# A top-32 attention and a cosine-gated layer: every step from one list with the first twenty units reordered, and the mask made from threshold minus score

## The chip, the cores and the metric

The kernel runs on one core of one Trainium2 chip. The metric is the time of one execution in device microseconds (us), as the median of several runs. The core has a matrix engine (TensorE, PE in the profile; its loads of stationary operands are listed as PEld), a vector engine (VectorE, DVE), a scalar engine (ScalarE, ACT), a general engine (GpSimd, POOL), and a sync engine (SyncE, SP) that here only issues DMAs. Each engine works through its own instructions in order and waits on semaphores for the others.

## The reference

Inputs are q, k and v of shape (8, 8, 576, 64), that is batch, heads, sequence, head size, and two weight matrices of 512 x 2048 and 2048 x 512. All arithmetic is float32. The reference, cut to what matters:

```python
scores = scale * np.matmul(q, k.transpose(0, 1, 3, 2))
kth = np.partition(scores, -32, axis=-1)[..., -32:-31]
scores = np.where(scores >= kth, scores, -1000000000.0)
scores = scores - np.max(scores, axis=-1, keepdims=True)
attn = np.exp(scores)
attn = attn / (np.sum(attn, axis=-1, keepdims=True) + 1e-09)
x = heads_joined(np.matmul(attn, v))      # (4608, 512)
h = x @ w_in                              # (4608, 2048)
return (h * np.cos(h)) @ w_out            # (4608, 512)
```

For each row of scores, only the 32 largest of 576 count; the softmax runs over these.

## The kernel before

**Units and blocks.** The 4608 token rows are cut into 36 blocks of 128. With the heads taken in four pairs, there are 144 units: unit n is block n // 4, head pair n % 4. A unit passes through these steps:

- Scores: PE multiplies q and k (L242), 448 columns into one PSUM tile (`sc`, two buffers) and 128 into a shared one (`rim`). ACT copies both to SBUF as `s` (`take_scores`, L253 and L257).
- Folding: a row's 576 scores are split in halves. DVE forms the maximum of each pair (`rest`, `fold_high`, L267); POOL forms the minimum as sum minus maximum on the integer bit patterns (`low`, L283 and L292). In units 8 to 10 (`BUSY`) DVE makes the minimum directly (`fold_now`, L275).
- Search: DVE takes the eight largest of a row at a time (MAX8, L359) and strikes them out (MATCH_REPLACE8, L364): four rounds on `rest`, two on `low`. Two small reductions merge the lists into the 32nd largest score, the threshold (L347, L352). They are done at the start of the next unit's search.
- Mask: two more small reductions on DVE make the negated threshold and the negated maximum (`bounds`, L372) and the distance of threshold and maximum (`distances`, L379), both between the maxima of the next unit's first round. ACT multiplies the distance by the scale (L386), masks (L388) and exponentiates with a running sum (L396). The mask is the function Prelu: a score minus the threshold stays as it is if it isn't negative, and is multiplied by 2^100 if it is, so that its exponential is zero.
- Sum and reciprocal on DVE (L404, L409).
- Transposition: POOL splits the words of `s` and the reciprocals into 16-bit halves (`split`, L419 and L421, into one buffer), SP writes them to DRAM (L450), and a transposing DMA reads them back into a ring of five (L456). The first four units are transposed by PE instead (`turn`, L438 to L446).

When the four units of a block are there, PE multiplies with v (`values`, L484) and DVE multiplies with the reciprocals (`take_values`, L500, L508), giving the block's x, transposed.

**The second layer, per block.** The first product takes 64 matmuls on PE (`ff1`, L562); ACT copies each PSUM bank twice (`take_first`, L576, L578); POOL reduces to the range of the sine (L598, L607); ACT takes the sine (L617); POOL multiplies (`gate`, L624); the second product takes 16 matmuls (`ff2`, L637); ACT copies the result (L647) and issues its store. A block has two chunks of g and x in SBUF: six buffers for g and three for x.

**Weights.** They arrive as 64-bit words and are decoded on the chip in 32 pieces of 128 x 512: a load of 512 KB (L120) into a buffer of g or x, two passes on ACT (L133, L136), a shift on DVE (L151, two adjacent pieces in one instruction where possible), and an addition on POOL (L160), after which the buffer is free.

**What sets the order.** A Python loop calls `slot` once for each unit, and each engine gets its instructions in the order in which the loop emits them. A slot holds the search of unit i, the mask and exponentials of unit i − 1, the split and transposition of unit i − 2, the scores of one or two units ahead, and pieces of the second layer. Which pieces those are is decided by `feed` from a small table (`plan`) and by tests on counters (`can_first`, `can_second`), which let the first product begin in slot 6 at the earliest and the second in slot 10. The loads of weights are issued on SP's queue in slots 0 to 5 and on ACT's queue in later ones. After the last unit, `drain` and `forward` emit what is left.

Of the kernel before, what the change touches and what calls it, by code (L numbers as in the profile page):

```python
# [17 lines left out]
P = 128  # L18
# [12 lines left out]
def kernel(  # L31
# [63 lines left out]
    BUSY = range(8, 11)  # L95
    ff = {"live": 0, "tick": 0, "now": 0, "end": False, "kind": 0, "half": 0, "open": 0, "late": False}

    wq = {"next": 0, "loaded": deque(), "second": deque(), "third": deque(), "done": 0, "ready": 0}

    def staged(spare=0):  # L100
        return sum(c[2] == spare for k in ("loaded", "second", "third") for c in wq[k])

    def load_weights(n, queue):
        for _ in range(n):
            i = wq["next"]
            if i >= len(chunks):
                return
            src, dst = chunks[i]
            if not DECODE:
                queue.dma_start(out=dst[0][:, dst[1]], in_=src)  # L110
                wq["next"] = wq["done"] = i + 1
                continue
            spare = i < 2 * NC + 10 and i % 2 == 1 and staged(1) < XB
            if spare:
                st = ffw.tile([P, CW, 2], I32, tag="x", name="st", bufs=XB)
            elif staged() + ff["live"] >= CHUNKS:
                return
            else:
                st = ffw.tile([P, CW, 2], I32, tag="g", name="st", bufs=CHUNKS)
            queue.dma_start(out=st.rearrange("p w i -> p (w i)"), in_=src)  # L120
            wq["loaded"].append((st, dst, int(spare)))
            wq["next"] = i + 1

# [3 lines left out]
    def decode_first(n):  # L127


        for _ in range(min(n, len(wq["loaded"]))):  # L130
            st, w, spare = wq["loaded"].popleft()
            lo, hi = st[:, :, 0], st[:, :, 1]
            nc.scalar.activation(  # L133
                out=w[0][:, w[1]], in_=hi.bitcast(F32), func=AF.Prelu, scale=2.0**-111, alpha=2.0**32
            )
            nc.scalar.mul(out=lo, in_=lo.bitcast(U32), mul=2.0**-29)  # L136
            wq["second"].append((st, w, spare))

    def decode_second(n):

        left = min(n, len(wq["second"]))
        while left:
            st, (w, c), spare = wq["second"].popleft()
            wq["third"].append((st, (w, c), spare))
            m = 1
            if left > 1 and wq["second"][0][1][0] is w:
                wq["third"].append(wq["second"].popleft())
                m = 2
            left -= m
            wi = w[:, c : c + m].bitcast(I32)  # L150
            nc.vector.tensor_scalar(  # L151
                out=wi, in0=wi, scalar1=3, scalar2=None, op0=ALU.logical_shift_left
            )

    def decode_third():

        while wq["third"]:
            st, w, _ = wq["third"].pop()
            wi = w[0][:, w[1]].bitcast(I32)
            nc.gpsimd.tensor_tensor(out=wi, in0=wi, in1=st[:, :, 0], op=ALU.add)  # L160
            wq["done"] += 1

# [69 lines left out]
    def scores(u):  # L235
        sc = u["sc"] = ps.tile([P, 2, 512], F32, tag="sc", name="sc", bufs=2)
        for to, k0, k1 in ((sc, 0, SB), (sc_ends[u["n"] % 2], SB, S)):
            for b, q0, rows, r0 in u["parts"]:
                for j in range(2):
                    d = slice(j * D, (j + 1) * D)  # L240
                    st = pairs[b, u["hp"]]
                    nc.tensor.matmul(  # L242
                        to[r0 : r0 + rows, rim_bank(r0, j) if k0 else place(u["hp"], j), 0 : k1 - k0],
                        st["q"][d, q0 : q0 + rows],
                        st["k"][d, k0:k1],
                        start=True,
                        stop=True,
                    )
# [61 lines left out]
    def topk_first(u, w):  # L310

        u["top"] = tops[u["n"] % len(tops)]
        if w:
            merge_first(w)
        if u["n"] not in BUSY:
            fold_sum(u)
        fold_high(u)
        if w:
            merge_second(w)
        if u["n"] in BUSY:  # L320
            fold_now(u)
        topk_round(u, 0, [lambda: bounds(w), lambda: distances(w)] if w else ())

    def topk_round(u, rnd, between=(), ahead=None):
        top, rest, lasts = u["top"], u["rest"], TOPK // 8 - 1
        end = TOPK - 1 - 8 * rnd
        at = top[:, :, end : end - 8 if rnd < lasts else None : -1, 0]
        search(
            at, rest[:, :, HS:S] if rnd == 0 else rest[:, :, 0:HS], rest[:, :, 0:HS], rnd < lasts,
            between if rnd < lasts else (),  # L330
        )
        if rnd < lasts:
            return
        del u["rest"]
        low = u.pop("low")
        for k in range(TOPK // 16):
            more = k < TOPK // 16 - 1
            if ahead and not more:
                ahead()
            search(top[:, :, 1 + 8 * k : 9 + 8 * k, 1], low, low, more, () if more else between)  # L340


# [14 lines left out]
    def search(to, src, rest, more, between=()):  # L357
        for j in range(2):
            nc.vector.max(to[:, j], src[:, j])  # L359
            if between:  # L360
                between[j]()
        if more:
            for j in range(2):
                nc.vector.match_replace(rest[:, j], to[:, j], src[:, j], NEG)  # L364

    def bounds(u):

        top = u.pop("top").rearrange("p j r i -> p j (r i)")
        end = 2 * TOPK
        less = u["less"] = top[:, :, end : end + 2]  # L370
        u["near"] = top[:, :, end - 1 : end + 1]
        nc.vector.tensor_reduce(  # L372
            out=less, in_=top[:, :, end - 2 : end].unsqueeze(3), axis=mybir.AxisListType.X,
            op=ALU.max, negate=True,
        )

    def distances(u):
        u["nd"] = small.tile([P, 2], F32, tag="nd", name="nd")
        nc.vector.tensor_reduce(  # L379
            out=u["nd"], in_=u.pop("near"), axis=mybir.AxisListType.X, op=ALU.add  # L380
        )

    def mask(u):

        s, less = u["s"], u.pop("less")
        nc.scalar.mul(out=u["nd"], in_=u["nd"], mul=SCALE)  # L386
        for j in range(2):
            nc.scalar.activation(  # L388
                out=s[:, j], in_=s[:, j], func=AF.Prelu, bias=less[:, j, 1:2], scale=1.0, alpha=FAR
            )  # L390

    def exponentials(u):
        s, nd = u["s"], u.pop("nd")
        den = u["den"] = dens[u["n"] % len(dens)]
        for j in range(2):
            nc.scalar.activation(  # L396
                out=s[:, j], in_=s[:, j], func=AF.Exp, bias=nd[:, j : j + 1], scale=SCALE,
                accum_out=den[:, j, 0:1],
            )
# [11 lines left out]
    def both(u):  # L411
        return [lambda: sums(u), lambda: reciprocal(u)] if u else ()

    def split(u):


        s = u.pop("s").rearrange("p j k -> p (j k)").bitcast(U16)
        halves = work.tile([P, 2, 2 * S + P], U16, tag="halves", name="halves", bufs=1)
        nc.gpsimd.tensor_copy(out=halves[:, :, 0 : 2 * S], in_=s.rearrange("p (k h) -> p h k", h=2))  # L419
        rden = u.pop("rden").bitcast(U16).rearrange("p (j h) -> p h j", h=2)  # L420
        nc.gpsimd.tensor_copy(  # L421
            out=halves[:, :, 2 * S :].rearrange("p h (j d) -> p h j d", j=2),
            in_=rden.unsqueeze(3).to_broadcast([P, 2, 2, D]),
        )
        u["halves"] = halves
# [4 lines left out]
    def turn(u):  # L430

        s = u.pop("s").rearrange("p j k -> p (j k)")
        pT = u["pT"] = ring[:, u["n"] % RING]
        for half in range(2):
            tt = ps.tile([P, 512], F32, tag="mm", name="tt", bufs=2)
            for c in range(NT):
                at = (half * NT + c) * P
                nc.tensor.transpose(tt[:, c * P : (c + 1) * P], s[:, at : at + P], ident)  # L438
            nc.scalar.copy(out=pT[:, half * NT : (half + 1) * NT], in_=tt.rearrange("p (c q) -> p c q", c=NT))  # L439
        at = 2 * NT * P  # L440
        nc.tensor.transpose(room[0][:, P : 2 * P], s[:, at : at + P], ident)
        rden = u.pop("rden")
# [3 lines left out]
        nc.scalar.copy(out=pT[:, 2 * NT :], in_=rim[:, :, 3 * P :])  # L446
# [43 lines left out]
    def take_values(us):  # L490
# [4 lines left out]
        while i < n:  # L495
            at, h = us[i]["n"] % RING, (hp + i) // 2
            m = 4 if n - i == 4 and at + 4 <= RING else 2 if at + 2 <= RING else 1
            if m > 1:
                o = rim[:, :, 2 * (S - SB) + h * P : 2 * (S - SB) + (h + m // 2) * P]
                nc.vector.tensor_tensor(  # L500
                    out=blk["xT"][:, hp + i : hp + i + m].rearrange("p (h b) q -> p h b q", b=2),
# [409 lines left out]
```

## Time and profile before

| what | value |
|---|---|
| median of 3 runs | 1413.1 us (1413.07 to 1413.49) |
| span of the profiled execution | 1410.6 us |
| busy in the span: PE, PEld | 1354.9 (96%), 976.6 (69%) |
| busy in the span: DVE, ACT, POOL | 1344.2 (95%), 1139.4 (81%), 1164.8 (83%) |
| largest groups on PE: first product L562, second product L637 | 540.0, 524.7 us |
| largest groups on DVE: L359 on `rest`, L364 on `rest` | 478.7, 376.4 us |
| mean of L372, L379 (DVE), x144 each | 140, 141 ns |
| mean of L386, L388, L396 (ACT) | 205, 762, 770 ns |

The profiled execution is one run under the hardware profiler; its span goes from the first instruction to the last, and the median of the runs lies 2.5 us above it. A line of a timeline reads: start in us from the span's start, duration, engine, source line, operation, output and input by the program's names, shapes and count, and in brackets the idle time of the engine before it and what ended that. A line of waits reads: engine and line that waited, what it waited for, the time in total, how often, the longest. "SPq" is a DMA issue on SP's queue.

### The profile page before, as it was taken

The page shows a single profiled execution, that of the slowest core. Times are in us where ns is not written, and L with a number is a line of the kernel's source. Part 1 is how long each engine was busy: PE and PEld are TensorE (multiplying, and loading weights), DVE is VectorE, ACT ScalarE, POOL GpSimd, SP SyncE. Part 2 cuts the span into 40 slices and gives each one's busy share as a digit, 9 for nine tenths or more (in the row PEclk, how much of TensorE's full clock was granted, in tenths as well). Part 3 has the DMA queues.
Part 4 walks back from the last instruction along what each step waited for, and adds up shares of the span by engine and source line. Part 5 has one row for each costly group of instructions (what it writes and reads, how often), then busy time and mean ns, then how long its engine had stood idle before and what let it go on. Part 6 is the DMA issues. An engine that isn't in the chain of part 4 may idle for free.

```text
span 1410.6 us, 32356 instructions
## 1 busy us (share of the span) xinstructions
PE 1354.9 (96%) x11264; PEld 976.6 (69%) x11264; DVE 1344.2 (95%) x5148; ACT 1139.4 (81%) x2043; POOL 1164.8 (83%) x804
## 2 busy tenths in 40 slices
PE   4568999999999999999999999999999999999998
PEld 2445777777777777777777777777777777777775
DVE  7999999999999999999999999999999999999931
ACT  6987888888888888888888888888888888888831
POOL 5778988898888888888888888888888888888810
PEclk7688999999999999999999999999999999999999
DMA  8566876767675575677666677666776666555540
GB/s 274 198 207 180 205 184 165 206 174 192 155 185 151 165 194 158 176 169 194 174 172 160 142 188 186 171 169 161 207 164 168 158 172 172 142 157 148 150 101 15
DMA packets 427443, 240.13 MB, mean 170 GB/s; under 512 B 375952, under 2 KB 392592, under 8 KB 427280
## 3 DMA queue, kind: packets, MB, share of 16 engines
q1 hardware_dynamic: 420720, 224.22, 60.8%
q10 hardware_dynamic: 6560, 13.85, 2.8%
q8 instruction: 88, 1.44, 0.4%
q14 instruction: 75, 0.61, 0.1%
HBM read 45.09 MB, written 101.19 MB: 104 GB/s over the span
## 4 chain that ended last, share of the span: by engine, by line
PE 83%; DVE 10%; ACT 4%; DMA 2%; SPq 0%; issue 0%; ACTq 0%; DVEq 0%
PE o L637 32%; PE mm L562 32%; PE rim L484 10%; PE sc L242 7%; DVE top L359 5%; DVE rest L364 3%; PE rim L242 2%; DMA st<-in_moe_w_in_dram 2%; DVE rest L267 1%; DVE low L364 1%; ACT s L396 1%; ACT st L136 1%; ACT s L388 1%; ACT w_out L133 0%; ACT w_in L133 0%; ACT ring L439 0%
## 5 line engine op out<-in xcount | busy, mean ns | idle before, releaser
L562 PEld LDWEIGHTS mm<-xT,w_in 128*128 128x128 f32 x4608 | 538.3, 192 | 70.8 <-issue 55.7
L562 PE MATMUL mm<-xT,w_in 128*128 128x128 f32 x4608 | 540.0, 276 | 2.2 <-DVE xT L500 1.3
L637 PE MATMUL o<-w_out,g 128*128 128x512 f32 x1152 | 524.7, 599 | 0.0
L359 DVE MAX8 top<-rest 128x8 f32<-128x288 f32 x1152 | 478.7, 451 | 0.0
L364 DVE MATCH_REPLACE8 rest<-top,rest 128x288 f32<-128x288 f32 x864 | 376.4, 443 | 0.0
L637 PEld LDWEIGHTS o<-w_out,g 128*128 128x128 f32 x1152 | 207.7, 190 | 219.5 <-issue 219.2
L419 POOL COPY halves<-s 128x2304 uint16<-128x2304 uint16 x140 | 294.6, 2104 | 51.4 <-ACT s L396 48.2
L359 DVE MAX8 top<-low 128x8 f32<-128x288 f32 x576 | 241.6, 448 | 0.4 <-POOL low L292 0.3
L396 ACT ACTIVATE s<-s,nd 128x576 f32<-128x576 f32 x288 | 220.6, 770 | 0.8
L292 POOL TENSOR_TENSOR low<-low,rest 128x576 int32<-128x576 int32 x141 | 199.3, 1413 | 11.0
L388 ACT ACTIVATE s<-s,top 128x576 f32<-128x576 f32 x288 | 205.7, 762 | 0.0
L283 POOL TENSOR_TENSOR low<-s 128x576 int32<-128x576 int32 x141 | 198.9, 1411 | 5.7 <-ACT s L259 5.7
L386 ACT ACTIVATE nd<-nd 128x2 f32<-128x2 f32 x144 | 29.5, 205 | 177.1 <-DVE nd L379 177.0
L607 POOL TENSOR_TENSOR x<-g,x 128x1024 f32<-128x1024 f32 x68 | 160.8, 2364 | 5.7
L624 POOL TENSOR_TENSOR g<-g,x 128x1024 f32<-128x1024 f32 x68 | 160.8, 2365 | 0.0
L242 PE MATMUL sc<-k,q 64*64 64x448 f32 (+1 forms) x1120 | 145.3, 564 | 15.7 <-DMA k<-in_k_dram 8.6
L484 PE MATMUL rim<-ring,v 128*64 128x128 f32 (+1 forms) x2560 | 138.1, 267 | 0.0
L484 PEld LDWEIGHTS rim<-ring,v 128*64 128x64 f32 x2560 | 129.0, 139 | 6.4 <-issue 5.9
L253 ACT COPY s<-sc 128x896 f32<-128x896 f32 (+1 forms) x144 | 128.5, 892 | 2.7 <-PE sc L242 2.7
L364 DVE MATCH_REPLACE8 low<-top,low 128x288 f32<-128x288 f32 x288 | 125.4, 443 | 0.0
L257 ACT COPY s<-rim 64x256 f32<-64x256 f32 (+1 forms) x280 | 103.0, 368 | 26.6 <-PE rim L484 24.9
L598 POOL TENSOR_SCALAR x<-x 128x1024 f32<-128x1024 int32 x68 | 71.2, 1047 | 63.5 <-ACT x L578 63.5
(56 smaller groups left out, 1272.3 us busy)
## 6 DMA issues: line engine op xcount, KB each, us to landing
rows<-halves SPq DMA_DIRECT2D x140, 640.0 KB, 3.5
out_dram<-ob ACTq DMA_DIRECT2D x36, 256.0 KB, 2.1
q<-in_q_dram SPq DMA_DIRECT2D x31, 288.0 KB, 4.3
st<-in_moe_w_in_dram SPq DMA_DIRECT2D x16, 512.0 KB, 6.9
v<-in_v_dram SPq DMA_DIRECT2D x32, 256.0 KB, 4.3
k<-in_k_dram SPq DMA_DIRECT2D x31, 144.0 KB, 4.2
k<-in_k_dram SPq DMA_DIRECT2D x32, 128.0 KB, 4.5
st<-in_moe_w_out_dram SPq DMA_DIRECT2D x8, 512.0 KB, 5.1
```

Of the source, the lines that this page charges most:

```text
L242: nc.tensor.matmul(to[r0 : r0 + rows, rim_bank(r0, j) if k0 else place(u["hp"], j), 0 : k1 - k0], st["q"][d, q0 : q0 + rows], st["k"][d, k ...
L283: nc.gpsimd.tensor_tensor(out=u["low"].bitcast(I32), in0=s[:, :, 0:HS], in1=s[:, :, HS:S], op=ALU.add)
L292: nc.gpsimd.tensor_tensor(out=low, in0=low, in1=u["rest"][:, :, HS:S].bitcast(I32), op=ALU.subtract)
L359: nc.vector.max(to[:, j], src[:, j])
L364: nc.vector.match_replace(rest[:, j], to[:, j], src[:, j], NEG)
L388: nc.scalar.activation(out=s[:, j], in_=s[:, j], func=AF.Prelu, bias=less[:, j, 1:2], scale=1.0, alpha=FAR)
L396: nc.scalar.activation(out=s[:, j], in_=s[:, j], func=AF.Exp, bias=nd[:, j : j + 1], scale=SCALE, accum_out=den[:, j, 0:1],)
L419: nc.gpsimd.tensor_copy(out=halves[:, :, 0 : 2 * S], in_=s.rearrange("p (k h) -> p h k", h=2))
L484: nc.tensor.matmul(to[d, r], lhsT, rhs, start=(bank, j) not in begun, stop=c == NT - 1 and u in us[-2:] and r0 + rows == P,)
L562: nc.tensor.matmul(mm[:, at : at + w], w_in[f // FC][:, c, (f % FC) * P : (f % FC + 1) * P], blk["xT"][:, c], start=c == 0, stop=c == NC - 1,)
L607: nc.gpsimd.tensor_tensor(out=x, in0=g, in1=x, op=ALU.subtract)
L637: nc.tensor.matmul(o, g[:, at : at + P], w_out[f], start=f == 0, stop=f == NF - 1)
```

## The change

The procedure that chose the order (`slot`, `plan`, `feed`, `can_first`, `can_second`, `drain`, `forward`) is gone. In its place stands one literal list of steps, which a loop calls one after the other; each token names a step and its unit, block or weight piece. `Sa.8` and `Sb.8` are the two parts of unit 8's scores, `K` the copies, `fs`, `fl`, `P0`, `P0b` the folds, `R0` to `R3`, `Q0`, `Q1` the rounds of the search, `M`, `E`, `C` the mask, the exponentials, and sum and reciprocal, `sp1`, `sp2`, `wr`, `tr` the split, write and transposition, `T1` to `T3e` those on PE, `V.4.8` and `X.4.8` the values of units 4 to 7 and their taking, `F1.b.i` and `F2.b.j` the eighths of block b's first and second product, `B1`, `A0`, `A`, `N`, `G` what lies between them, `L`, `D1`, `D2`, `D3` the load and the three decoding steps of a weight piece.

From unit 20 on the list gives PE the same instructions in the same order as before. In the first twenty units the order is new: among other things, the values of block 0 stand in the middle of slot 7 (before: in slot 5, with the first product in slot 6); the first three eighths of block 0's second product stand before the values of block 1 (before: behind them); the split of a unit may stand right behind its exponentials; units 15 and 17 are scored before units 14 and 16. All weight loads are issued on SP's queue, among the writes and transposing DMAs of units 4 to 10. Each weight piece is shifted on its own: 32 shifts of 512 columns instead of 13 of 1024 and 6 of 512.

The mask is Prelu of threshold minus score: negative for the scores that stay, which are multiplied by 2^-100, while the others stay as they are; the exponential's scale undoes both. `bounds` is not needed for it and is gone, `distances` subtracts, and the multiplication of the distance stands behind the masks.

The diff, cut to its core:

```diff
-    def bounds(u):
-        top = u.pop("top").rearrange("p j r i -> p j (r i)")
-        ...
-        nc.vector.tensor_reduce(
-            out=less, in_=top[:, :, end - 2 : end].unsqueeze(3), axis=mybir.AxisListType.X,
-            op=ALU.max, negate=True,
-        )
     def distances(u):
+        top = u["top"]
         u["nd"] = small.tile([P, 2], F32, tag="nd", name="nd")
-        nc.vector.tensor_reduce(
-            out=u["nd"], in_=u.pop("near"), axis=mybir.AxisListType.X, op=ALU.add
+        nc.vector.tensor_tensor(
+            out=u["nd"], in0=top[:, :, TOPK - 1, 1], in1=top[:, :, TOPK - 1, 0], op=ALU.subtract
         )
     def mask(u):
-        s, less = u["s"], u.pop("less")
-        nc.scalar.mul(out=u["nd"], in_=u["nd"], mul=SCALE)
+        s, top = u["s"], u.pop("top")
         for j in range(2):
             nc.scalar.activation(
-                out=s[:, j], in_=s[:, j], func=AF.Prelu, bias=less[:, j, 1:2], scale=1.0, alpha=FAR
+                out=s[:, j], in_=s[:, j], func=AF.Prelu, bias=top[:, j, TOPK - 1, 1:2], scale=-1.0,
+                alpha=1.0 / FAR,
             )
+        nc.scalar.mul(out=u["nd"], in_=u["nd"], mul=SCALE)
     def exponentials(u):
         ...
-                out=s[:, j], in_=s[:, j], func=AF.Exp, bias=nd[:, j : j + 1], scale=SCALE,
+                out=s[:, j], in_=s[:, j], func=AF.Exp, bias=nd[:, j : j + 1], scale=-SCALE * FAR,
...
-    def decode_second(n):
-        ...
-            wi = w[:, c : c + m].bitcast(I32)
+    def decode_second(k):
+        w, c = chunks[k][1]
+        wi = w[:, c].bitcast(I32)
...
-    def slot(i, u, w, x, z):
-        ...
+    for t in """
+...
+R0.7 R1.7 D1.24 L.25.g D1.23 D1.25 D2.24 D3.24 sp2.5 V.0.4 M.6 E.6 VV.4 X.0.4 Sa.9 L.26.g D1.22
+Sb.9 R2.7 tr.4 D2.23 F1.0.0 F1.0.1 R3.7 Q0.7 Q1.7 K.8 P0.8 P0b.8 R0.8 D3.15 F1.0.2 D3.23 wr.5
+D1.26 M.7 E.7 B1.0.0 Sa.10 D2.26 L.27.g D2.25 Sb.10 sp1.6 D3.25 F1.0.3 F1.0.4 F1.0.5 C.6 sp2.6
+B1.0.1 VV.5 VV.6 A0.0.0 D2.22 R1.8 R2.8 R3.8 tr.5 F1.0.6 wr.6 A.0.0 C.7 sp1.7 sp2.7 wr.7 Q0.8
+Q1.8 D3.20 K.9 P0.9 P0b.9 D1.27 B1.0.2 K.10 D2.27 N.0.0 R0.9 M.8 Sa.11 Sb.11 R1.9 R2.9 F1.0.7
+R3.9 Q0.9 Q1.9 P0.10 P0b.10 K.11 D3.22 L.28.g G.0.0 F2.0.0 D3.26 F2.0.1 F2.0.2 E.8 L.29.g sp1.8
+B1.0.3 R0.10 tr.6 C.8 Sa.12 A0.0.1 Sb.12 tr.7 sp2.8 M.9 E.9 V.4.8 A.0.1 R1.10 L.30.g R2.10 D1.30
+wr.8 tr.8 R3.10 C.9 Q0.10 D3.27 X.4.8 F1.1.0 Q1.10 P0.11 sp1.9 sp2.9 N.0.1 G.0.1 D2.30 D3.30
+...
+fl.22 R1.22 R2.22 F1.3.7 Sa.23 Sb.23 Sa.24 Sb.24 V.16.20 M.21 B1.3.3 E.21 K.23 R3.22 Q0.22
+...
+""".split():
+    ...
+    for step, *of in order:
+        steps[step](*of)
```

## The prediction

> **What bounds the kernel now.** I read the page first (share of each engine, the 40 slices), then a table of busy times by stretches, then the waits of PE (the matrix engine) and of DVE (the vector engine) before and after 140 us, then the timelines around single steps.
>
> ```profile
> PE 1354.9 (96%) x11264; PEld 976.6 (69%) x11264; DVE 1344.2 (95%) x5148; ACT 1139.4 (81%) x2043; POOL 1164.8 (83%) x804
> PE   4568999999999999999999999999999999999998
> DVE  7999999999999999999999999999999999999931
> PEclk7688999999999999999999999999999999999999
> ```
>
> Two engines are full almost to the end. Only the first four slices (each 35.3 us) show PE below 9. The table of stretches says the same in microseconds (its columns: busy time and instructions of PE, PEld, DVE, ACT and POOL, then the granted PE clock, the DMA share, GB/s):
>
> ```profile
> 35.00:70.00 35.00, 20.77 (x147) 15.30 (x146) 33.46 (x124) 31.51 (x66) 26.83 (x22) 0.60 0.58 198
> 70.00:105.00 35.00, 22.81 (x185) 18.12 (x183) 35.00 (x129) 29.95 (x58) 26.77 (x21) 0.84 0.71 213
> 105.00:140.00 35.00, 28.56 (x235) 19.57 (x236) 34.11 (x130) 27.65 (x50) 28.53 (x20) 0.87 0.65 180
> 188.17:224.87 36.70, 36.70 (x313) 26.43 (x308) 36.70 (x144) 30.82 (x57) 32.33 (x23) 1.00 0.68 169
> ```
>
> The last row is one block of four units in the steady part. Which of the two full engines sets it is told by the waits:
>
> ```profile
> PE mm L562 <- ACT x L578: 0.3, 1, 0.3
> PE sc L242 <- DVE low L275: 7.1, 3, 3.3
> ACT nd L386 <- DVE nd L379: 177.0, 135, 2.9
> ```
>
> The first row is all that PE waited from 140 us to the end: 0.3 us. The second is one of its waits before 140 us, where its idle time is 140 − (16.13 + 20.77 + 22.81 + 28.56) = 51.7 us. The third is the scalar engine ACT, over the whole run, waiting for the distances before it may mask. So after 140 us PE decides: its pieces for one block in the chain of waits are 4 x 3.57 (first product) + 4 x 3.63 (second) + 4.08 (values) + 4 x 0.96 (scores) = 36.7, which is the pitch of the values step (703.10 and each 36.70 before and behind it). DVE's slots sum to 3 x 8.99 + 9.67 = 36.64: it is 0.06 behind, within a hair. Before 140 us DVE decides, as it is idle there for some 10 us only, 6 of them at its start.
>
> The profiled span is 1410.6, the median of the runs 1413.1: 2.5 us lie around the span, and I carry them over.
>
> **The change part by part.**
>
> *Bounds removed, mask turned round.* One DVE instruction goes per unit (L372). It lasts 140 ns, but beside its neighbours it takes 0.055 to 0.06: in the timeline it starts 0.38 after the maximum before it, and the next maximum starts 0.05 later. 144 x 0.06 = 8.6 us of DVE. The sum in L379 becomes a subtraction of the same width: nothing. After 140 us PE has no wait that these 8.6 us could shorten, so there they are worth nothing; they leave DVE at 36.4 against 36.70. In units 0 to 19 they count: 20 x 0.06 = 1.2. On ACT the multiplication L386 moves behind the two masks, which now wait only for the threshold (L352), not for bounds and distances: one maximum + 0.06 + one maximum + 0.06 earlier, 0.36 + 0.06 + 0.36 + 0.06 = 0.84. Everything behind the mask on ACT (exponentials, copies of the first product) can come that much earlier.
>
> *Weight shifts one chunk at a time.* Before: 13 of 1024 columns at 0.60 and 6 of 512 at 0.34 = 9.8; after: 32 x 0.34 = 10.9. Costs DVE 1.1, all of it before 140 us.
>
> *DVE's lead.* Summed by hand with 8.93 for a slot, 0.34 for a shift, 0.66 for a direct fold and 0.68 for taking the values, from the first fold at 6.97, slot 13 of the new order starts at 136.9, against 139.81: 2.9 earlier, most of it the 2.65 us that DVE waits in its first slots for copies and no longer should. To unit 20 it gains another 7 x 0.06 = 0.4. New waits (shifts of chunks whose loads are just in, scores copied just in time, small reductions side by side) I bound between 0 and 3 from the nearest rows, DVE's own waits of 0.3 to 1.5 us in this stretch, and take 1.4. Lead at unit 20: 2.9 + 0.4 − 1.4 = 1.9.
>
> *PE's lead.* Values of block 0 are moved up and three of eight pairs of block 0's second product (6 x 0.90 = 5.4 us) are put before the values of block 1, into a stretch where PE is idle:
>
> ```profile
> 109.37 0.70 PE L242 MATMUL rim<-k,q 64*64 64x128 f32 x8 [7.11 <-ACT s L257]
> 111.50 1.77 PE L242 MATMUL sc<-k,q 64*64 64x448 f32 x8 [1.42 <-DVE low L275]
> 113.44 1.00 PE L484 MATMUL rim<-ring,v_tail 64*64 64x128 f32 x16
> ```
>
> They need the gate of chunk 0 on POOL. In the new order of POOL it stands behind unit 7's split and two weight additions (2.55), and takes 2.36. That split ends at 101.43 in the trace; I put it 0.9 earlier by DVE's lead, at 100.5, and the gate's end at 100.5 + 2.55 + 2.36 = 105.4. Then 105.4 + 5.4 = 110.9, scores 0.96, and the values of block 1 start at 111.9 instead of 113.44. The next values, of block 2, start in the trace at 151.44, held by a transposing DMA:
>
> ```profile
> 143.15 0.34 SPq L450 DMA_DIRECT2D rows<-halves  x1
> 146.25 2.95 SPq L456 DMA_TRANSPOSE ring<-rows  x1
> ```
>
> It lands about 5.0 after its issue, at 151.2. Unit 11's split now stands right behind its exponentials, its reciprocal inside the fourth round of unit 12, not at that unit's end: the write can go at about 135 instead of 143.15, and the transfer lands at about 143.3. What holds PE then is its own work: I put the values of block 2 at 146.2, 5.2 earlier, less 0.96 for scores of one unit that are now behind it: 4.2. From unit 20 on the instructions of PE are in the same order as before, to the last, and a shift of its start is a shift of its end.
>
> *Which lead counts.* In the steady part PE may run ahead of DVE only as far as ACT delivers the first product's copies. At 717.34 such a copy ends (L578, 716.66 + 0.68) and PE wants the bank at 717.84: slack 0.50. The earlier mask adds 0.84, so 1.34. So PE's gain is the smaller of 4.2 and DVE's lead plus this slack, 1.9 + 1.34 = 3.2. Taken: 3.3, as the transposes, with about 2 us to spare (landing 222.8, values 224.87), allow up to 3.9. Span 1410.6 − 3.3 = 1407.3; with the 2.5, **1409.8**.
>
> *Queues passed.* Eight weight loads (512 KB each, 0.33 us to issue) go from ACT's queue to SP's, before and between the writes and transposes of units 4 to 10. ACT saves 8 x 0.33 = 2.7 us of issuing, not on the path. On SP each load waits for its staging buffer, and whatever stands behind waits too; the rival below prices that.
>
> *Two rules beside rows.* The trace first: PE idle for 7.11 us before 109.37 is followed by a granted clock of 0.50 from 104 to 112 and 0.72 from 112 to 116; a gap of 2.38 us before 101.27 left it at 1.00. The Trainium skill (TensorE: Matmul & The Clock Gate, Part 1: The HAM clock gate) has the clock halved after one idle window of about 3.4 us that runs freely, and restored after as long a busy one. The gap that I see before the moved pairs, about 2.9 us from 102.5 to 105.4, is between the two rows. By the row of 2.38 it costs nothing, which I take, being nearer; by the row of 7.11 about 4.6 us run at half, 2.3 us lost. By the page's rule it would be nothing or 1.7. Second, the skill (DMA: Bandwidth & Descriptors, Issuing engines are not separate DMA queues) says that another issuing engine saves only the time of issuing. By it the move of the loads would cost 8 x 0.33 on SP and no more; it leaves out the buffer waits, which no run here prices yet.
>
> **The rivals.**
>
> *Half clock (or a late block 1) eats the gain.* The gap before the second product's first pairs is over 3 us, PE runs them at half clock, values of block 1 come 2.3 later. For it: the clock falls to 0.50 or 0.60 in each early stretch. Against: PE works steadily from the earlier values on. Time: 1409.8 + 2.3 = 1412.1, no measurable change.
>
> *The SP queue, slower.* Loads 28 and 29 stand before the transposes of units 6 and 7 and wait for POOL's additions of chunks 20 and 22, which stand behind unit 7's split. Transpose 6 (2.7 to issue) then goes at 103.1, transpose 7 at 105.8; in the trace they land 5.0 to 7.1 after issue, so 110.8 to 112.9, against 111.9 wanted. Up to there it costs 1. If unit 6's write also slips behind transpose 5, a whole round is added: write 3.5, split 2.5, transpose 2.7 = 8.7, and values, DVE's taking of them and all later slots are 8.7 late, less the 0.7 or so to spare. Time 1409.8 + 8.0 = 1417.8. Each us that transpose 7 lands after 111.9 is then a us lost: from 115.2 on (3.3 late) the kernel is slower than before, from 118 measurably. Against: POOL has idle time of 5.28 us before 106.71.
>
> *DVE was the bound.* Then 8.6 of bounds come off in full: 1413.1 − 8.6 = 1404.5. For: DVE 139.74 busy of 140. Against: PE's 0.3 us of waits.
>
> **How the numbers follow.** About 2.8 us (0.2%) is what a measurement of this kernel can tell from none. Forecast 0.56, its own range 1407.5 (lead without new waits) to 1410.6; half clock or late block 0.22; SP queue 0.17; DVE 0.05. Faster: 0.05 + most of the forecast, 0.51 = 0.56. Slower: 0.17 and a tail of the second case, 0.19. The rest, 0.25, within. The range leaves out the far half of the SP case and the DVE case's tail: 1404.5 to 1416.5.
>
> **What would show it.** Right: slot 13 (L347's new line) starts near 137 to 138, values of blocks 1, 2, 3 near 111.9, 146.2, 182.9; block pitch 36.70 behind them; no wait of ACT's mask for the distances; end of PE 3 us earlier at the same distance behind. Wrong: a pitch other than 36.7 (the bound was not PE); transpose 7 landing after 113; clock 0.5 from 103 to 111; PE waits for L578's line after 200 us of more than 1 us in sum.

## The result and the profile after

The changed kernel takes 1479.4 us (median of 5 runs, 1477.7 to 1480.3) against 1413.1: 66 us more, a ratio of 1.0461 (95% interval 1.0446 to 1.0476). Its profiled execution has a span of 1476.4. The forecast was 1409.8, faster.

The page of the changed kernel, busy times and slices of two engines:

```profile
PE 1372.8 (93%) x11264; PEld 974.9 (66%) x11264; DVE 1413.6 (96%) x5017; ACT 1141.5 (77%) x2043; POOL 1170.4 (79%) x804
PE   4467899999999999999999999999999999999998
DVE  7999999999999999999999999999999999999941
```

DVE lost 131 instructions and got 69 us busier (1344.2 before). Its share of the chain that ended last, 10% before, is now:

```profile
DVE 90%; PE 7%; issue 1%; ACT 0%; SPq 0%; DMA 0%; DVEq 0%
```

So DVE is the bound, in the steady part too. In a block there (same table of stretches as before), PE is no longer full:

```profile
700.00:738.10 38.10, 37.08 (x305) 26.31 (x305) 38.10 (x140) 30.69 (x56) 32.35 (x23) 1.00 0.69 178
```

The pitch of the values steps is 38.07 to 38.22, not 36.70. Among the groups of DVE by line and shape (busy time, mean ns), two have changed out of proportion:

```profile
L332 DVE TENSOR_TENSOR nd<-top 128x2 f32<-128x2 f32 x144 | 84.7, 588 | 0.1
L121 DVE TENSOR_SCALAR w_out<-w_out 128x512 int32<-128x512 int32 x16 | 16.8, 1056 | 0.0
L121 DVE TENSOR_SCALAR w_in<-w_in 128x512 int32<-128x512 int32 x16 | 9.7, 629 | 0.5 <-ACT w_in L113 0.5
```

The first is the subtraction that makes the distances: 588 ns for two columns, where the reduction it replaces took 141. The others are the weight shifts: 26.5 us in all, where I had put 32 x 0.34 = 10.9. The last column, idle time before the instruction, is near zero: whatever the instructions wait for is counted as their own busy time. The durations of one kind are far apart (minimum, median, maximum in ns):

```profile
L332 DVE TENSOR_TENSOR nd<-top x144: 142/580/1361, 18.4 to 1410.7; 128x2 f32<-128x2 f32 x144
```

The timelines of DVE and of POOL around one subtraction show what it is:

```profile
705.01 0.46 DVE L322 MAX8 top<-rest 128x8 f32<-128x288 f32 x1
705.39 0.58 DVE L332 TENSOR_TENSOR nd<-top 128x2 f32<-128x2 f32 x1
705.89 0.45 DVE L322 MAX8 top<-rest 128x8 f32<-128x288 f32 x1
```

```profile
704.54 1.41 POOL L247 TENSOR_TENSOR low<-s 128x576 int32<-128x576 int32 x1
706.03 1.42 POOL L256 TENSOR_TENSOR low<-low,rest 128x576 int32<-128x576 int32 x1
```

The subtraction ends at 705.97; POOL's running instruction ended at 704.54 + 1.41 = 705.95. In the whole trace POOL is in the middle of an instruction at 140 of the 144 subtractions, and all 140 end within 0.05 us of that instruction's end; in the other four POOL is idle or has just ended, and they last 0.14 to 0.16. A shift behaves alike, with its own work behind the wait:

```profile
85.53 2.26 DVE L121 TENSOR_SCALAR w_out<-w_out 128x512 int32<-128x512 int32 x1
```

```profile
85.41 2.10 POOL L368 COPY halves<-s 128x2304 uint16<-128x2304 uint16 x1
```

POOL ends at 87.51, the shift at 87.79. Of the 32 shifts, 18 start beside a running POOL instruction, and all 18 end 0.28 to 0.29 behind its end; the other 14 last 0.40 to 0.43. So theory 1: these two kinds of DVE instruction don't run beside an instruction of POOL; they wait until it has ended. Its rival, theory 2: the new order is what costs, and the long rows are its symptom.

### The profile page after: what moved, and what is told of

The parts are those of the page before. It is cut to its first block, busy times and chain, and to the rows that moved or that the text cites. A ratio compares the mean times of both kernels' runs of the same rounds, so it can differ in the third digit from the quotient of the medians.

```text
span 1476.4 us, 32313 instructions
## 1 busy us (share of the span) xinstructions
PE 1372.8 (93%) x11264; PEld 974.9 (66%) x11264; DVE 1413.6 (96%) x5017; ACT 1141.5 (77%) x2043; POOL 1170.4 (79%) x804
## 4 chain that ended last, share of the span: by engine, by line
DVE 90%; PE 7%; issue 1%; ACT 0%; SPq 0%; DMA 0%; DVEq 0%
DVE top L322 41%; DVE rest L327 24%; DVE low L327 8%; DVE rest L231 7%; DVE nd L332 5%; PE o L553 3%; PE mm L507 3%; DVE xT L473 1%; DVE w_out L121 1%; DVE top L308 1%; DVE top L313 1%; DVE rden L363 1%; PE rim L451 1%; DVE w_in L121 1%; DVE den L358 1%
## 5 line engine op out<-in xcount | busy, mean ns | idle before, releaser
L206 PE MATMUL sc<-k,q 64*64 64x448 f32 (+1 forms) x1120 | 148.3, 572 | 59.2 <-DVE rest L231 53.5
L374 POOL COPY halves<-rden 128x256 uint16<-128x256 uint16 x140 | 57.2, 409 | 107.8 <-DVE rden L363 106.9
L231 DVE TENSOR_TENSOR rest<-sc,s 128x576 f32<-128x576 f32 x144 | 107.6, 747 | 6.6 <-ACT s L223 6.4
```

Of the source, the lines that this page charges most:

```text
L231: nc.vector.tensor_tensor(out=u["rest"][:, :, HS:S], in0=sc[:, :, 0:HS], in1=s[:, :, HS:S], op=ALU.max)
```

## The experiments

Each is timed beside the kernel before, whose median on these chips was 1413.2 to 1413.6.

**1. The exchange of one instruction in the old order.**

```diff
-        nc.vector.tensor_reduce(
-            out=u["nd"], in_=u.pop("near"), axis=mybir.AxisListType.X, op=ALU.add
-        )
+        near = u.pop("near")
+        nc.vector.tensor_tensor(out=u["nd"], in0=near[:, :, 0], in1=near[:, :, 1], op=ALU.add)
```

> The kernel before with one instruction exchanged: the distances (L379) are made by a two-input addition of the same two columns, not by a reduction over the pair. Theory 1 (a DVE instruction with two inputs in SBUF waits until the instruction that POOL is running has ended): at the places where L379 stands before, POOL's running instruction has 0 to 2.3 us left, 0.6 in the mean, so the instruction lasts about 0.5 to 0.7 us instead of 0.14, DVE's block goes from 36.65 to about 38.4, past PE's 36.70, and the time rises by 45 to 75 us, to 1458 to 1488. Theory 2 (the new order is what costs, a two-column instruction costs 0.14 in either form): 1411 to 1415.

Measured: 1482.3 us, ratio 1.0489 (1.0473 to 1.0504). One instruction per unit, of the same two columns, costs as much as the whole change. The row of its group:

```profile
L380 DVE TENSOR_TENSOR nd<-top 128x2 f32<-128x2 f32 x144 | 94.9, 659 | 0.0
```

The block pitch is 38.70. Theory 2 is out for the larger part.

**2. The new order and the new mask, distances by two reductions.** `bounds` and `distances` of before put back; the mask still waits for the threshold alone.

```diff
-        nc.vector.tensor_tensor(
-            out=u["nd"], in0=top[:, :, TOPK - 1, 1], in1=top[:, :, TOPK - 1, 0], op=ALU.subtract
+        nc.vector.tensor_reduce(
+            out=u["nd"], in_=u.pop("near"), axis=mybir.AxisListType.X, op=ALU.add
         )
```

> The changed kernel with the distances made as before, by two reductions with one input each (bounds and distances), while the mask stays the new one that waits for the threshold alone. Theory 1: the instruction is back at 0.14, the block pitch is PE's 36.70 again, some 45 to 55 us come off; what stays is the late start, caused by single weight shifts that also wait for POOL: 1422 to 1432. Theory 2: nothing much comes off, 1470 to 1482.

Measured: 1430.9 us, 1.0118 (1.0102 to 1.0135): 48.5 less than the changed kernel, with two instructions in place of one. The distances are back at 141 ns and the pitch at 36.70, so PE is the bound again behind the start:

```profile
PE mm L516 <- ACT x L531: 0.3, 1, 0.3
```

This is all that PE waited from 200 us on. What is left, 17.7 us, lies in the start: the values of block 4 begin at 243.72, before at 224.87.

**3 and 4. The mask.** Run 3 is run 2 with the whole mask of before; run 4 is the kernel before with the new mask, distances by reductions. The core of run 4's edit; run 3's is the reverse:

```diff
-                out=s[:, j], in_=s[:, j], func=AF.Prelu, bias=less[:, j, 1:2], scale=1.0, alpha=FAR
+                out=s[:, j], in_=s[:, j], func=AF.Prelu, bias=top[:, j, TOPK - 1, 1:2], scale=-1.0,
+                alpha=1.0 / FAR,
```

> The changed kernel with the whole mask of before (bounds, distances, the multiplication ahead of the masks): the new order alone. Theory 1: within 3 us of the run with the new mask and reductions, 1422 to 1434, as ACT has the 0.84 us to spare. Theory 2 (the order costs): 1470 to 1482.

> The kernel before with the new mask (threshold minus score, the multiplication behind the masks) but distances still by the two reductions. Theory 1: the mask itself is worth nothing measurable, 1410.5 to 1413.5. Theory 2, and a third by which the turned mask is dear (a negative scale, other values for the exponential): the third would give 5 us or more above 1413.

Measured: 1429.9 (1.0114, 1.0099 to 1.0129) and 1413.0 (0.9998, 0.9988 to 1.0007). The turned mask is worth nothing in either order, and costs nothing.

**5. Without the shifts**, on top of run 2. The weights are then not decoded; the run tells of time alone.

```diff
-        nc.vector.tensor_scalar(
-            out=wi, in0=wi, scalar1=3, scalar2=None, op0=ALU.logical_shift_left
-        )
```

> The changed kernel with distances by reductions, and the shifts of the weights (L121 on DVE) left out: their part of the decoding is not done. Theory 1 (the late start comes from the shifts, which wait until POOL's running instruction has ended: 28.3 us in 26 rows of the trace where before they took 11.0): DVE gets both the 17 of waiting and the 11 of shifting back, and PE's own work sets the start: 1404 to 1412. Theory 2 (the late start is the queue on SP, the clock or the order of the steps): 1420 or more.

Measured: 1410.6, 0.9980 (0.9970 to 0.9989). With the shifts gone, the late start is gone too. But this run takes their work away too, so it does not yet tell waiting from work.

**6. Single shifts in the old order.**

```diff
-            if left > 1 and wq["second"][0][1][0] is w:
+            if False and left > 1 and wq["second"][0][1][0] is w:
```

> The kernel before with every shift made for one piece alone, 32 instead of 19, at the same places. Theory 1: there POOL has nothing to run while the shifts run, as its next instruction is the addition that needs them, so they do not wait; they cost 13 starts more, 1.1 us of DVE: 1413 to 1416. Theory 2 (a single shift is dear by itself, 1.05 us as in the changed kernel's w_out rows): 1422 or more.

Measured: 1413.1, 0.9996 (0.9987 to 1.0005). A single shift is not dear. In the order of before, a shift stands where POOL's next instruction is the addition that needs this very shift, so POOL is idle when most of them start: in this run at 29 of the 32, which last 0.41 to 0.43. The other three start beside the end of a POOL instruction and end 0.28 behind it; the longest lasts 1.22. In the kernel before it is the same: the 1024-column shift had a median of 0.68, and the longest, 0.82, is one of two that started beside a POOL instruction and ended 0.55 behind it.

**7. Shifts regrouped in the new order.** Run 2 with, in units 0 to 17, shifts and additions put together behind round 2, adjacent pieces paired, and POOL's folds moved up. A piece of the new list:

```diff
+... R2.2 D2.4.2 D2.6.2 D2.8.2 D3.4 D3.5 D3.6 D3.7 D3.8 D3.9 R3.2 ...
```

> The changed kernel with distances by reductions, and in units 0 to 17 the shifts and additions of the weight pieces whose first step is done put together behind round 2 (two adjacent pieces in one shift), the folds on POOL directly behind the first one on DVE: the places of the kernel before, all else in the new order. Theory 1: shifts take 11 to 15 us in sum again and the time comes to 1409 to 1417. Theory 2 (the order of the other steps costs): 1422 or more.

Measured: 1430.5, 1.0118 (1.0105 to 1.0132): a miss for theory 1's time, though the shifts take 14.6 us in sum as it expected. DVE now waits elsewhere, for decoding steps of ACT, which itself waits 10.9 and 12.2 us for loads, and for PE:

```profile
DVE w_out L121 <- ACT w_out L113: 4.0, 1, 4.0
DVE xT L475 <- PE rim L460: 3.9, 1, 3.9
DVE w_in L121 <- ACT w_in L113: 3.8, 2, 3.3
```

A regrouping that makes waits of its own separates nothing; hence run 9.

**8. Distances on ACT in the old order.**

```diff
+            nc.scalar.activation(
+                out=nd[:, j : j + 1], in_=top[:, j, TOPK - 1, 0:1], func=AF.Identity,
+                bias=top[:, j, TOPK - 1, 1:2], scale=-1.0,
+            )
```

> The kernel before with the new mask, without bounds and without distances on DVE: ACT makes the distance with one instruction for each head, threshold minus maximum, of 0.2 us. DVE has 2 x 0.06 x 144 = 17 us less to do. If PE is the bound behind 140 us, only the start can gain, 13 slots x 0.12 = 1.6: 1410.5 to 1413.5. If DVE was the bound: 1396 to 1404. If ACT has not the 0.4 us per unit: above 1416.

Measured: 1413.7, 1.0002 (0.9994 to 1.0011). Two DVE instructions less in each unit give nothing: with the old order and no waits for POOL, DVE's small instructions are not on the path, and the gain of 1.6 that I allowed the start did not appear. The fold of slot 13 comes even later, at 141.43 against 139.95 before; ACT has two instructions more in each unit here, but whether they cause this is not shown.

**9. A stand-in for the shift**, on top of run 2: a reduction at the same place. The weights are again not decoded.

```diff
-        nc.vector.tensor_scalar(
-            out=wi, in0=wi, scalar1=3, scalar2=None, op0=ALU.logical_shift_left
-        )
+        nc.vector.tensor_reduce(out=wf[:, 0:1], in_=wf[:, 0:256], axis=mybir.AxisListType.X, op=ALU.max)
```

> The changed kernel with distances by reductions, and in place of each of the 32 weight shifts a reduction of 256 columns of the same piece on DVE (so the shift is not done): the same place, the same dependences, about the same 0.34 us, but one input and a kind of instruction that in no trace here waited for POOL. Theory 1 (the waits of the shifts for POOL are the late start, not their work and not the new order): the rows last 0.3 to 0.4 us each whatever POOL runs, and the time is within 4 us of the run without shifts, 1409 to 1414.5. Theory 2 (the run without shifts gained because DVE had 11 us less work, and the new order with shifts that don't wait is still late): 1417 to 1425.

Measured: 1418.4, 1.0035 (1.0021 to 1.0049). That lies between runs 2 and 5, and in the range of theory 2: shifts that don't wait still leave the new order late. The reductions never wait, as theory 1 had it; 22 of the 32 start beside a running POOL instruction, and all last 0.40 to 0.42 (minimum, median, maximum of half of them):

```profile
L121 DVE TENSOR_REDUCE w_out<-w_out x16: 398/409/414, 54.1 to 140.3; 128x1 f32<-128x256 f32 x16
```

So the waiting of the shifts is worth 1430.9 − 1418.4 = 12.5, their work 7.8 more (to run 5), and the new order without the waiting is still about 5 behind the kernel before. A wait of PE in the values of block 1 says where some of that is:

```profile
113.95 0.96 PE L458 MATMUL rim<-ring,v_tail 64*64 64x128 f32 x12
116.91 0.69 PE L458 MATMUL rim<-ring,v_tail 64*64 64x128 f32 x4 [2.00 <-DMA ring<-rows]
```

**10. Transposing DMAs ahead of the loads**, on top of run 9.

```diff
-... wr.7 ... L.28.g ... L.29.g ... tr.6 ... tr.7 ... V.4.8
+... tr.6 wr.7 tr.7 ... L.28.g ... L.29.g ... V.4.8
```

> As the run with stand-in reductions in place of the shifts (the shift is not done), and on SP's queue the transposing DMA of unit 6 stands before the write of unit 7, that of unit 7 directly behind that write, and the two weight loads 28 and 29 behind both; before, the loads and the write stood in front. In the stand-in run unit 7's rows landed at 116.9, PE waited 2.0 for them inside the values of block 1, and these ran on at 116.9, where the kernel before has 113.4. Theory A (the queue on SP holds the start back): they land before 113.95, no wait, and the time falls by 2 to 4 us, to 1414.5 to 1416.5. Theory B (the values of block 1 are late for other reasons and later waits take the gain): 1417 to 1420.

Measured: 1415.4, 1.0018 (1.0009 to 1.0027): 3.0 less, as theory A had it. The values of block 1 start at 112.87 without a wait. On SP's timeline of this run the transposition of unit 7 now stands ahead of the loads:

```profile
105.48 2.75 SPq L430 DMA_TRANSPOSE ring<-rows  x1
108.33 1.48 SPq L105 DMA_DIRECT2D st<-in_moe_w_out_dram  x3
```

About 2 us against before remain, with one more such wait of PE for a transposed unit, of 2.4 us, between 105 and 240 us; I did not follow that up, so the cause of these 2 us stays open.

No run that does all the work is measurably faster than the kernel before, so there is no better version to show.

## Why the prediction was wrong

The 66 us, from the medians: 48.5 for the subtraction with two inputs (changed kernel to run 2), 12.5 for the shifts' waiting (run 2 to 9), 3.0 for the queue on SP (run 9 to 10), 2 for the rest of the new order.

**The step that failed** is the half sentence "The sum in L379 becomes a subtraction of the same width: nothing". I priced the instruction by its width; its price is set by what it reads and by what POOL is doing. 588 − 141 = 447 ns for 144 units are 64 us, less 8.6 for the bounds: 56 of DVE's time, of which the 0.06 per block that DVE had to spare takes 2. By the rows: DVE's slot went from 8.99 to 9.37, a block from 36.64 to 38.1, which is 1.4 past PE's 36.70; 36 blocks of that are 50 us, near the 48.5 measured.

The trace of before held a row of this kind, and I did not look for it. Nearly all its two-input DVE instructions have one input in PSUM; the fold (L267) lasts 746 to 758 ns in all 144 rows whatever POOL runs. But in the last four chunks DVE itself subtracts x from g (L596), both in SBUF:

```profile
L596 DVE TENSOR_TENSOR x<-g,x x4: 1215/1225/2083, 1348.8 to 1394.4; 128x1024 f32<-128x1024 f32 x4
1348.85 2.08 DVE L596 TENSOR_TENSOR x<-g,x 128x1024 f32<-128x1024 f32 x1
```

```profile
1347.75 2.11 POOL L419 COPY halves<-s 128x2304 uint16<-128x2304 uint16 x1 [3.55 <-ACT s L396]
1349.80 1.39 POOL L421 COPY halves<-rden 128x256 uint16<-128x256 uint16 x1
```

Three of the four run while POOL is idle and last 1.22. The first starts beside POOL's split, lasts 2.08 and ends 1.07 behind it. POOL's next copy lasts 1.39 and ends 0.26 behind the subtraction; the other 139 copies of its kind last 0.39 to 0.42, so here POOL waited in its turn. From this row the new form had to be bounded by what is left of POOL's running instruction, up to 2.4 us.

A rule was there to be weighed: the Trainium skill (SBUF — State Buffer, Who interferes with whom) says that a DVE instruction with two SBUF inputs contends with a GpSimd instruction that reads SBUF, that a `tensor_scalar` instruction (the shift is one) can contend too, and that reductions on this chip never do. All three agree with the rows here: 140 of 140 subtractions, the shifts' 0.28 behind POOL's end, and 398 to 419 ns for the stand-ins. I weighed two other rules instead.

**Shifts: a mis-sized term.** 32 x 0.34 = 10.9 was put; the rows sum to 26.5. The 0.34 is right where POOL idles, as run 6 shows, and it mostly idled before because its next instruction waited for the shift. The new list parts shifts from their additions, so POOL is busy at 18 of the 32.

**DVE's lead.** Slot 13 was to start at 136.9, or 138.3 with the new waits; it starts at 160.6, and even in run 10, where neither shifts nor distances wait for POOL, at 140.15, against 139.81 before. Run 10 still makes the bounds (13 x 0.06 = 0.8 by my price) and has one new wait of 1.1, for a decoding step; with these the sum of 2.9 gives 138.8. So about 1.3 of the lead is not there, and which of its terms is wrong is not shown.

**PE's lead.** Here the steps hold if DVE has its 11 us of shifts off: in run 5 the values of blocks 2 and 3 start at 145.61 and 182.85 (predicted 146.2 and 182.9), and the span is 1407.5 (predicted 1407.3). That is no credit for the forecast, which had counted the shifts. (The smaller of 4.2 and 3.2 is 3.2; the prediction took 3.3.)

**What was right.** PE is the bound wherever DVE does not wait for POOL (pitch 36.70 in runs 2 and 10); the early mask is worth nothing there (runs 3, 4); the bounds' 8.6 us are worth nothing (run 8). The mask of the changed kernel no longer waits for the distances but for the threshold (and once, 3.2 us, for POOL), as this row of the waits from 140 us on has it:

```profile
ACT s L340 <- DVE top L313: 213.9, 128, 2.3
```

**The rivals.** The queue on SP was real but small: in run 9 unit 7's rows landed 4 to 6 us after my 110.8 to 112.9, and moving them forward gave 3.0. The rule that I had cited, by which another issuing engine saves only issue time (the Trainium skill, DMA: Bandwidth & Descriptors, Issuing engines are not separate DMA queues), does not cover this: what cost was the order within one queue. The half clock did not come: in run 9 PE idles 2.93 us before the moved pairs, the granted clock is 1.00 from 104 to 112, and the twelve matmuls take 5.42, as put; in the changed kernel it is 1.00 from 104 to 128. "DVE was the bound" came out with the opposite sign: DVE was 0.06 per block behind, and the change added 1.5 to it. I had seen that hair's breadth and used it only in the one direction; a rival in which DVE gets slower was missing.

## What to carry to other kernels

- Before an instruction is exchanged for one "of the same width", list what each reads and through what: here, one two-column vector instruction with two SBUF inputs cost 48 us in 1479, because it stood beside a POOL that is 80% busy. If the old form looks clumsy (two reductions where a subtraction would do), look for the reason in the rows of its neighbours.
- Where two engines are within 1% of each other, a change to the second one needs a price from above, not only from below.
- A wait of this kind shows as a longer busy time, not as idle time: compare minimum, median and maximum of a group, and where they spread, set its ends beside the ends of the other engines' instructions. Here one row of four, 2083 against 1225, held the warning before the change.

## What the runs showed of the hardware that was not expected

- A two-column DVE subtraction with both inputs in SBUF lasts 0.14 us with POOL idle and up to 1.36 beside it, and ends within 0.05 us of POOL's instruction. With one input in PSUM (the fold, 746 to 758 ns in 144 rows) or in the form of a reduction (131 to 158 ns in the 144 distances of run 2, 139 of them beside POOL), no such wait is seen.
- A DVE shift of 512 columns lasts 0.40 to 0.43 alone and up to 2.52 beside POOL; it ends some 0.28 behind POOL's instruction.
- Where POOL itself waits for the shift, the two seldom meet (3 of 32 in run 6): the same 32 shifts cost nothing measurable in the old order (run 6) and, by their waiting alone, 12.5 us in the new one.
